# Moving the low parts of the weights to GpSimd, with a constant tensor for 1e-9 and one copy on ScalarE

## The chip, the cores and the metric

The kernel runs on one core of one Trainium2 chip. The metric is the device time of one launch in microseconds (us); lower is better. A core has TensorE (PE in the profile) for matrix products, VectorE (DVE), ScalarE (ACT) and GpSimd (POOL) for element-wise work, and SyncE (SP), which here issues the DMA transfers. Each engine works through its own instructions in order; semaphores make one engine wait for another. SBUF is the on-chip memory that all engines use, PSUM the memory that TensorE writes its results to.

## The reference

```python
# 8 batches, 8 heads, 576 rows, head size 64
k_p = k.reshape(8, 8, 72, 8, 64).mean(axis=3)      # keys pooled by 8
v_p = v.reshape(8, 8, 72, 8, 64).mean(axis=3)
scores = (1 / sqrt(64)) * q @ k_p.transpose(0, 1, 3, 2)
scores = scores - max(scores, axis=-1, keepdims=True)
attn = exp(scores)
attn = attn / (sum(attn, axis=-1, keepdims=True) + 1e-09)
x = (attn @ v_p)                                   # rearranged to 4608 x 512
h = x @ w_in                                       # 512 x 2048
g = maximum(0.01 * h, h)
out = g @ w_out                                    # 2048 x 512, float32
```

The two weights arrive as 64-bit floats. The kernel makes 32-bit values of them on the chip, and it keeps nearly the whole float32 precision in its matrix products by splitting each operand into a high part (rounded to TensorE's fp32r format) and a low part (what the rounding left).

## The kernel before, in words

**Tiling.** The 4608 rows of x are nine chunks of 512 rows. The hidden width of 2048 is sixteen groups f of 128. For a chunk and a group, twelve matmuls build h in a PSUM tile `ph` (L851 high weight by high x, L852 high weight by low x, L853 low weight by high x, four times each). ScalarE applies the leaky relu to it (L856) and rounds it to `gh` (L859), VectorE subtracts for the low part `gl` (L860), and twelve more matmuls add g times the second weight to four output tiles `acc` (L877, L878, L879). The second product of a group comes two groups after the first.

**Attention.** A tile of 128 rows of q is transposed by TensorE to `pq` (L467) and copied from PSUM to `qT` (for the first batch by VectorE at L470 where the tile number t is above 1, by ScalarE at L472 otherwise). `pss` (L495) holds scores of four heads; VectorE takes the row maximum (L503, into the tile `red`), ScalarE the exponentials and their sums (L505, `e`), VectorE adds 1e-9 to the sums and takes the reciprocal (L516 and L517 in `norm_unit` for the first three batches, L535 and L536 in `norm_via` for the rest), and GpSimd multiplies (L519, L523, L539, L545; `at`). TensorE transposes this (`pp`, L587), ScalarE and VectorE split it in parts (`pT_hi` L589, `pT_rem` L590, `pT_lo` L593, L597), and TensorE multiplies with the pooled v (`pa`, L612 to L615). The low part of v that belongs to it, and `kT`, the pooled keys (L405 and L406), come once for a batch. GpSimd does the pooling sums of later batches (L254, L261) on the raw tiles that SyncE's queue loads; the rows that don't fit a tile go through `kremraw` and `vremraw` to `v_parts` (L433 on ScalarE, L434 on VectorE).

**Weights.** There are 32 conversions: for each group f one of the first weight (i = 0) and one of the second (i = 1), each of 128 partitions by 512 values. `head` reads the two halves of the 64-bit words from SBUF: ScalarE rescales them in place (L198, L199), and VectorE puts the result together in a tile `w_t` with three instructions (L200, L201, L204). `tail` then has ScalarE write the rounded high part (L208) and VectorE the low part, `w_t` minus the high part (L209). The tile `w_t` lies in PSUM while the list `banks` has more than one entry, which is so for the first six conversions (f = 0, 1, 2), and in SBUF in a pool of three buffers for the other 26. The steps of the next conversion come between the head and the tail of one, and a conversion's `bits` go on to the DMA of a group four later (`stage`). The conversions come in stretches: the first six with the first batch's attention, the next 13 (f = 3 to 8, and one of f = 9) up to and beside the first pass over chunk 0, and the other 13 beside the second half of chunk 1 and what follows it.

**What sets the order.** TensorE's order is written out by hand: the string `FIRST` for the first batch, and then a loop over `runs` (chunk 0 with groups 0 to 7, the two halves of chunk 1 with groups 0 to 7, chunk 1 with groups 8 to 15, chunk 0 with groups 8 to 15, and then each chunk with all groups), which spreads the attention of the following batches and the steps of the conversions between the matmuls. The other engines get their order from a scheduler, which works with estimated times; a changed estimate or engine can therefore also change the order of instructions that the edit doesn't name.

Of the kernel before, what the change touches and what calls it, by code (L numbers as in the profile page):

```python
# [10 lines left out]
F32 = mybir.dt.float32  # L11
# [4 lines left out]
ALU = mybir.AluOpType  # L16
# [8 lines left out]
def tile_pooled_attention_ffn(  # L25
# [9 lines left out]
    nc = tc.nc  # L35

    P = 128
# [36 lines left out]
    const = ctx.enter_context(tc.tile_pool(name="const", bufs=1))  # L74
# [63 lines left out]
        "rem": const.tile([P, PMAX], F32R, name="pT_rem"),  # L138
    }

    warm = const.tile([P, 1], F32, name="warm")
    nc.gpsimd.memset(warm, 0.0)
    nc.scalar.activation(warm, warm, AF.Exp)
# [11 lines left out]
    def spare(f, i, shape, dtype, name):  # L155

        return wts.tile(shape, dtype, tag=f"w{i}_{f}", name=name)

    def stage(f):

        if f >= NF:
            return
        slot = NF - 1 if f == NF - 2 else NF - 1 - f % SPARE
        for i in range(2):
            shape = [P, DM, 2]
            if slot > f:
                t = spare(slot, i, shape, I32, f"w{i}_bits{f}")
            else:
                t = two.tile(shape, I32, tag="raw", name=f"w{i}_bits{f}")
            if i == 0:  # L170
                nc.sync.dma_start(
                    t.rearrange("p (k f) w -> p k f w", k=NK), w_in[:, :, f * P : (f + 1) * P, :]
                )
            else:
                nc.sync.dma_start(t, w_out[:, f, :, :])
            bits[i, f] = t

    def convert(i, f):

        st = {}  # L180

        def head():
            b = bits.pop((i, f))
            low, high = b[:, :, 0], b[:, :, 1]
            ws[i, f] = spare(f, i, [P, 2, DM], F32R, f"w{i}_{f}")

            if len(banks) > 1:
                k = 2 + (2 * f + i) % 2
                t = ps_acc.tile([P, DM], I32, tag=f"acc{k}", name=f"w{i}_t{f}")
            else:  # L190
                t = five.tile([P, DM], I32, tag="o", name=f"w{i}_t{f}")
            st["w"] = t.bitcast(F32)

            after = casts[-BEHIND] if len(casts) >= BEHIND else anchor.get("act")
            with tc.issue_after(after.ins) if after else nullcontext():
                nc.scalar.mul(high.bitcast(F32), high.bitcast(F32), 2.0**-112)  # L198
                nc.scalar.activation(low, low.bitcast(U32), AF.Copy, scale=2.0**-29)  # L199
            nc.vector.tensor_scalar(t, high, -0x80000000, None, op0=ALU.bitwise_and)  # L200
            nc.vector.scalar_tensor_tensor(  # L201
                t, high, 3, t, op0=ALU.logical_shift_left, op1=ALU.bitwise_or
            )
            nc.vector.tensor_tensor(t, t, low, op=ALU.add)  # L204

        def tail():
            w, t = ws[i, f], st["w"]
            nc.scalar.copy(w[:, 0, :], t)  # L208
            nc.vector.tensor_tensor(w[:, 1, :], t, w[:, 0, :].bitcast(F32), op=ALU.subtract)  # L209
            if i == 1:  # L210
                stage(f + SPARE)

        return head, tail

    banks = [(ps_a, "a"), (ps_a, "a"), (ps_h, "h"), (ps_h, "h")]
# [229 lines left out]
    def q_tile(b, t):  # L447
        qT = two.tile([P, NK, P], F32, tag="qT", name=f"qT{b}_{t}")
        if tiles[b][t][1] < P:
            nc.gpsimd.memset(qT[:, :, tiles[b][t][1] :], 0.0)  # L450
        return qT

    def q_unit(b, t, qr):
        n = tiles[b][t][1]
        if b > 1:

            qT = q_tile(b, t)
            m = n // 32
            blocks = qr.rearrange("a h d -> a (h d)")[:, : NK * n]
            nc.vector.transpose(  # L460
                qT[:, :, :n].rearrange("k p (s g) -> k g p s", g=m),
                blocks.rearrange("a (g p d) -> a g p d", g=m, p=NK),
            )
            return qT
        pq = bank(b, f"pq{b}_{t}")
        for p in range(NK):
            nc.tensor.transpose(pq[:, p, :n], qr[:n, 2 * p : 2 * p + 2, :], ident[:n, :n])  # L467
        qT = q_tile(b, t)
        if b == 0 and t > 1:
            nc.vector.tensor_copy(qT[:, :, :n], pq[:, :, :n])  # L470
        else:
            nc.scalar.copy(qT[:, :, :n], pq[:, :, :n])  # L472
        return qT
# [6 lines left out]
    def wide_at(b, t, nm):  # L480
        return b == 0 and (nm, t) in WIDE
# [31 lines left out]
    def norm_unit(b, t, g, e, sm):  # L513
        n = tiles[b][t][1]
        eng = nc.vector if b == 0 and t in NORM_DVE else nc.gpsimd
        nc.vector.tensor_scalar_add(sm[:n], sm[:n], 1e-9)  # L516
        nc.vector.reciprocal(sm[:n], sm[:n])  # L517
        at = wide(b, t, g, "at", [3, P]) if wide_at(b, t, "at") else three.tile([P, 3, P], F32, tag="at", name=f"at{b}_{t}_{g}")
        eng.tensor_tensor(  # L519
            at[:n, 0:2, :].rearrange("a i (h s) -> a (i h) s", h=2), e[:n, :, 0:MAIN],  # L520
            sm[:n].unsqueeze(2).broadcast_to([n, 4, MAIN]), op=ALU.mult,
        )
        ins = eng.tensor_tensor(  # L523
            at[:n, 2, :].rearrange("a (h c s) -> a h c s", h=4, c=4),
            e[:n, :, MAIN:].unsqueeze(2).broadcast_to([n, 4, 4, REM]),
            sm[:n].unsqueeze(2).unsqueeze(3).broadcast_to([n, 4, 4, REM]), op=ALU.mult,
        )
        if b == 0:
            anchor[eng] = ins
        return at  # L530

    def norm_via(b, t, g, e, sm):

        n = tiles[b][t][1]
        nc.vector.tensor_scalar_add(sm[:n], sm[:n], 1e-9)  # L535
        nc.vector.reciprocal(sm[:n], sm[:n])  # L536
        at = three.tile([P, 4, 3, 32], F32, tag="at", name=f"at{b}_{t}_{g}")
        for i in range(2):
            nc.gpsimd.tensor_tensor(  # L539
                at[:n, :, i, :].rearrange("a (h f) j -> a h f j", h=2),  # L540
                e[:n, 2 * i : 2 * i + 2, 0:MAIN].rearrange("a h (f j) -> a h f j", f=2),
                sm[:n, 2 * i : 2 * i + 2].unsqueeze(2).unsqueeze(3).broadcast_to([n, 2, 2, 32]),
                op=ALU.mult,
            )
        nc.gpsimd.tensor_tensor(  # L545
            at[:n, :, 2, :].rearrange("a h (c s) -> a h c s", c=4),
            e[:n, :, MAIN:].unsqueeze(2).broadcast_to([n, 4, 4, REM]),
            sm[:n].unsqueeze(2).unsqueeze(3).broadcast_to([n, 4, 4, REM]), op=ALU.mult,
        )
        rows = dram.tile([4, n, 96], F32, name=f"rows{b}_{t}_{g}")  # L550
        nc.sync.dma_start(
            rows.rearrange("x a y -> a x y"), at[:n].rearrange("a x i j -> a x (i j)")
        )
        return rows
# [518 lines left out]
```

## Time and profile before

| | |
|---|---|
| time, median of 3 runs | 936.06 us (935.46 to 937.29) |
| the profiled execution, its own time | 936.69 us |
| its span, first to last instruction | 934.9 us |
| TensorE (PE) busy | 903.4 us, 97% of the span |
| VectorE (DVE) busy | 424.9 us, 45% |
| ScalarE (ACT) busy | 417.2 us, 45% |
| GpSimd (POOL) busy | 183.9 us, 20% |
| mean granted TensorE clock | 0.991 |

The profile is of one execution; 1.8 us of its time lie outside the span. "Busy" counts the time in which an engine had an instruction under way. In the timelines a row has the start of the first instruction in us, the time taken in us, the engine, the line of the kernel and the operation, what is written and read, the shape, and how many instructions of the kind the row joins ("x2"). In brackets, where there is one, stands how long the engine was idle before it, and what it waited for. A "PEld" row is the load of a stationary operand, an "SPq" row the issue of a transfer. The granted clock is a share of TensorE's full speed.

### The profile page before, as it was taken

The numbers are of one execution on the slowest core, as the hardware profiler recorded it, in microseconds if no ns is written. First come the engines' busy times: TensorE is split into PE (matmuls) and PEld (weight loads), VectorE is DVE, ScalarE is ACT, GpSimd is POOL, SyncE is SP. The second block draws the span as 40 slices with busy tenths as digits, with TensorE's granted clock in tenths as the row PEclk, the third lists the DMA queues.
The fourth block names the chain that finished last, engine by engine and source line by source line (L and its number), as shares of the span: only waits on it lengthen the run. The fifth ranks groups of instructions, "written<-read, shape, count | busy, mean of one in ns | idle before, by whom it ended". The sixth has DMA issues, their size and how long they took to land.

```text
span 934.9 us, 12770 instructions
## 1 busy us (share of the span) xinstructions
PE 903.4 (97%) x4364; PEld 757.0 (81%) x4364; DVE 424.9 (45%) x986; ACT 417.2 (45%) x1375; POOL 183.9 (20%) x354
## 2 busy tenths in 40 slices
PE   5599999999999999999999999999999999999998
PEld 4478888888888888888888888888888888888886
DVE  6999469435343453436235534454345422421111
ACT  5788567435343444434344434443544333323221
POOL 4501110355023500313023212420211011000000
PEclk9799999999999999999999999999999999999999
DMA  9955231245032422514144404421322011101001
GB/s 264 320 181 169 61 76 46 52 116 143 12 96 53 108 72 54 125 35 110 33 90 115 107 7 106 98 71 32 102 50 61 26 62 31 39 1 46 1 1 45
DMA packets 127328, 75.14 MB, mean 80 GB/s; under 512 B 93472, under 2 KB 112672, under 8 KB 127264
## 3 DMA queue, kind: packets, MB, share of 16 engines
q1 hardware_dynamic: 127120, 74.21, 30.2%
q8 instruction: 34, 0.56, 0.2%
q14 instruction: 30, 0.25, 0.1%
q10 hardware_dynamic: 144, 0.13, 0.0%
HBM read 54.98 MB, written 19.33 MB: 79 GB/s over the span
## 4 chain that ended last, share of the span: by engine, by line
PE 86%; ACT 3%; DVE 3%; DMA 2%; POOL 1%; issue 1%; SPq 0%; POOLq 0%; DVEq 0%; ACTq 0%
PE acc L877 13%; PE acc L879 13%; PE acc L878 13%; PE ph L851 13%; PE ph L853 13%; PE ph L852 13%; PE pss L495 4%; PE pa L615 1%; PE pa L612 1%; PE pa L613 1%; PE pa L614 1%; ACT e L505 1%; PE pp L587 1%; DMA blocks<-rows 1%; DMA k0raw<-in_k_dram 0%
## 5 line engine op out<-in xcount | busy, mean ns | idle before, releaser
L851 PE MATMUL ph<-xh,w 128*128 128x512 f32 (+1 forms) x608 | 235.6, 387 | 0.1
L853 PE MATMUL ph<-xh,w 128*128 128x512 f32 (+1 forms) x608 | 231.1, 380 | 0.0
L852 PE MATMUL ph<-xl,w 128*128 128x512 f32 (+1 forms) x608 | 230.7, 379 | 0.0
L877 PE MATMUL acc<-w,gh 128*128 128x512 f32 x576 | 230.3, 400 | 0.0
L879 PE MATMUL acc<-w,gl 128*128 128x512 f32 x576 | 225.1, 391 | 0.0
L878 PE MATMUL acc<-w,gh 128*128 128x512 f32 x576 | 224.8, 390 | 0.0
L856 ACT ACTIVATE ph<-ph 128x512 f32<-128x512 f32 (+1 forms) x152 | 85.4, 562 | 263.3 <-PE ph L853 263.1
L860 DVE TENSOR_TENSOR gl<-ph,gh 128x512 fp32r<-128x512 f32 (+1 forms) x152 | 100.2, 659 | 224.8 <-ACT gh L859 224.2
L505 ACT ACTIVATE e<-pss,red 128x72 f32<-128x72 f32 (+1 forms) x320 | 98.2, 322 | 96.9 <-DVE red L503 96.8
L853 PEld LDWEIGHTS ph<-xh,w 128*128 128x128 f32 x608 | 114.5, 188 | 22.0
L851 PEld LDWEIGHTS ph<-xh,w 128*128 128x128 f32 x608 | 114.8, 189 | 20.8 <-DVE gl L860 0.5
L852 PEld LDWEIGHTS ph<-xl,w 128*128 128x128 f32 x608 | 114.8, 189 | 20.0
L879 PEld LDWEIGHTS acc<-w,gl 128*128 128x128 f32 x576 | 108.1, 188 | 23.3
L877 PEld LDWEIGHTS acc<-w,gh 128*128 128x128 f32 x576 | 108.3, 188 | 20.4
L878 PEld LDWEIGHTS acc<-w,gh 128*128 128x128 f32 x576 | 108.3, 188 | 20.0
L539 POOL TENSOR_TENSOR at<-e,red 128x128 f32<-128x128 f32 (+1 forms) x100 | 37.9, 400 | 320.1 <-DVE red L536 177.4
L859 ACT CAST gh<-ph 128x512 fp32r<-128x512 f32 (+1 forms) x152 | 86.0, 566 | 4.0
L503 DVE TENSOR_REDUCE red<-pss 128x4 f32<-128x288 f32 (+1 forms) x80 | 36.2, 453 | 81.0 <-PE pss L495 78.1
L505 ACT ACTIVATION_READ_ACCUMULATOR e<-pss,red 128x1 f32 (+1 forms) x320 | 65.8, 206 | 0.0
L495 PEld LDWEIGHTS pss<-kT,qT 128*128 128x128 f32 x320 | 50.0, 195 | 9.8 <-DVE qT L470 4.2
L495 PE MATMUL pss<-kT,qT 128*128 128x144 f32 x320 | 53.4, 293 | 3.8 <-DVE qT L470 3.8
L567 DVE STREAM_TRANSPOSE pp<-blocks 128x384 f32<-128x384 f32 (+1 forms) x50 | 36.5, 760 | 37.1 <-DMA blocks<-rows 36.7
(120 smaller groups left out, 822.0 us busy)
## 6 DMA issues: line engine op xcount, KB each, us to landing
out_dram<-o SPq DMA_DIRECT2D x34, 256.0 KB, 2.4
w_bits<-in_moe_w_in_dram SPq DMA_DIRECT2D x16, 512.0 KB, 10.5
w_bits<-in_moe_w_out_dram SPq DMA_DIRECT2D x16, 512.0 KB, 4.9
rows<-at SPq DMA_DIRECT2D x40, 192.0 KB, 3.1
blocks<-rows SPq DMA_DIRECT2D x40, 192.0 KB, 2.6
q<-in_q_dram SPq DMA_DIRECT2D x96, 64.0 KB, 2.5
k0raw<-in_k_dram SPq DMA_DIRECT2D x12, 256.0 KB, 3.9
k1raw<-in_k_dram SPq DMA_DIRECT2D x12, 256.0 KB, 3.8
```

The costliest lines, as they stand in the source:

```text
L495: nc.tensor.matmul(sc[:, 2 * SP * i : 2 * SP * (i + 1)], qT[:, p, :], kT[:, p, :, :].rearrange("d i s -> d (i s)"), start=True, stop=True,)
L505: ins = nc.scalar.activation(e[:n, h, :], scv[:n, h, :], AF.Exp, bias=mx[:n, h : h + 1], accum_out=sm[:n, h : h + 1],)
L539: nc.gpsimd.tensor_tensor(at[:n, :, i, :].rearrange("a (h f) j -> a h f j", h=2), e[:n, 2 * i : 2 * i + 2, 0:MAIN].rearrange("a h (f j) -> ...
L851: nc.tensor.matmul(ph, w[:, 0, ks], xh[kk][:, r], start=kk == 0, stop=False)
L852: nc.tensor.matmul(ph, w[:, 0, ks], xl[kk][:, r], start=False, stop=False)
L853: nc.tensor.matmul(ph, w[:, 1, ks], xh[kk][:, r], start=False, stop=kk == NK - 1)
L856: nc.scalar.activation(ph, ph, AF.Prelu, alpha=0.01)
L859: casts.append(nc.scalar.copy(gh, ph))
L860: nc.vector.tensor_tensor(gl, ph, gh.bitcast(F32), op=ALU.subtract)
L877: nc.tensor.matmul(a, gh[:, r], hi, start=first, stop=False)
L878: nc.tensor.matmul(a, gh[:, r], lo, start=False, stop=False)
L879: nc.tensor.matmul(a, gl[:, r], hi, start=False, stop=last)
```

## The change

There are three edits.

1. The low part of a weight (L209) is subtracted by GpSimd where `w_t` lies in SBUF, by VectorE where it lies in PSUM. This moves 26 of 32 instructions of 128 by 512 from VectorE to GpSimd.
2. A constant tile `tiny` of 128 by 4 is filled with 1e-9 at the start by GpSimd, and the 80 additions of 1e-9 (30 at L516, 50 at L535) become an addition of two tensors in place of a tensor and a number.
3. The copy of q's transpose of the first batch's last tile (t = 4, 64 rows) goes to ScalarE (L472) in place of VectorE (L470). Tiles 2 and 3 stay on VectorE.

```diff
+    tiny = const.tile([P, 4], F32, name="tiny")
+    nc.gpsimd.memset(tiny, 1e-9)
...
             ws[i, f] = spare(f, i, [P, 2, DM], F32R, f"w{i}_{f}")
 
+            st["eng"] = nc.vector if len(banks) > 1 else nc.gpsimd
             if len(banks) > 1:
                 k = 2 + (2 * f + i) % 2
                 t = ps_acc.tile([P, DM], I32, tag=f"acc{k}", name=f"w{i}_t{f}")
...
             nc.scalar.copy(w[:, 0, :], t)
-            nc.vector.tensor_tensor(w[:, 1, :], t, w[:, 0, :].bitcast(F32), op=ALU.subtract)
+            st["eng"].tensor_tensor(w[:, 1, :], t, w[:, 0, :].bitcast(F32), op=ALU.subtract)
...
-        if b == 0 and t > 1:
+        if b == 0 and 1 < t < 4:
             nc.vector.tensor_copy(qT[:, :, :n], pq[:, :, :n])
         else:
             nc.scalar.copy(qT[:, :, :n], pq[:, :, :n])
...
-        nc.vector.tensor_scalar_add(sm[:n], sm[:n], 1e-9)
+        nc.vector.tensor_tensor(sm[:n], sm[:n], tiny[:n], op=ALU.add)
```

The last pair of lines stands twice, at L516 and L535. The lines of the changed kernel lie four further down than those of the kernel before (L209 is L213, L503 is L507, L856 is L860); the text uses the numbers of before unless it says otherwise. The orders of TensorE and SyncE are the same in both kernels. The others change at several places, of which three are shown. Names such as `w_3_603` are the tile (the weight part of group 3) and a running number that differs by two between the kernels.

The first place is VectorE's and ScalarE's order around the copy of q, some 45 us into the program. VectorE before:

```order
L204 ISA w_t_565<-w_bits_179,w_t_565 128x1024
L630 TENSOR_TENSOR xl_2_403<-pa_1_2_536,xh_2_399 128x256
L434 SCALAR_TENSOR_TENSOR v_parts<-vremsum_164,v_parts 32x64 x2
L200 TENSOR_SCALAR w_t_514<-w_bits_177 128x512
L470 COPY qT_4_559<-pq_4_554 128x4x64
L630 TENSOR_TENSOR xl_3_404<-pa_1_3_541,xh_3_400 128x256
L209 TENSOR_TENSOR w_2_564<-w_t_565,w_2_564 128x512
L201 SCALAR_TENSOR_TENSOR w_t_514<-w_bits_177,w_t_514 128x512
L503 TENSOR_REDUCE red_4_0_577<-pss_4_0_573 64x4
```

ScalarE of the changed kernel there, and behind it VectorE of the changed kernel:

```order
L633 CAST xh_2_401<-pa_1_2_536 128x256
L437 ACTIVATE v_parts<-vremsum_166 32x64 x2
L633 CAST xh_3_402<-pa_1_3_543 128x256
L476 COPY qT_4_561<-pq_4_556 128x4x64
L212 CAST w_2_566<-w_t_567 128x512
L509 ACTIVATE e_4_0_578,red_4_0_579<-pss_4_0_575,red_4_0_579 64x72 x4
```

```order
L204 TENSOR_SCALAR w_t_516<-w_bits_179 128x512
L634 TENSOR_TENSOR xl_3_406<-pa_1_3_543,xh_3_402 128x256
L213 TENSOR_TENSOR w_2_566<-w_t_567,w_2_566 128x512
L507 TENSOR_REDUCE red_4_0_579<-pss_4_0_575 64x4
L205 SCALAR_TENSOR_TENSOR w_t_516<-w_bits_179,w_t_516 128x512
```

The copy has left VectorE's row and stands on ScalarE directly behind the last `xh`, ahead of the cast of `w_2`. On VectorE the maximum `red_4_0` has moved ahead of the conversion's L201.

The second place is where the subtractions of groups 3 and 4 now stand on GpSimd, between the multiplications of the first batch and those of the second. GpSimd before:

```order
L519 TENSOR_TENSOR at_4_1_600<-e_4_1_586,red_4_1_587 64x256
L523 TENSOR_TENSOR at_4_1_600<-e_4_1_586,red_4_1_587 64x128
L519 TENSOR_TENSOR at_0_0_829<-e_0_0_793,red_0_0_794 128x256
L523 TENSOR_TENSOR at_0_0_829<-e_0_0_793,red_0_0_794 128x128
L519 TENSOR_TENSOR at_0_1_925<-e_0_1_867,red_0_1_868 128x256
```

GpSimd of the changed kernel:

```order
L523 TENSOR_TENSOR at_4_1_602<-e_4_1_588,red_4_1_589 64x256
L527 TENSOR_TENSOR at_4_1_602<-e_4_1_588,red_4_1_589 64x128
L213 TENSOR_TENSOR w_3_605<-w_t_606,w_3_605 128x512
L213 TENSOR_TENSOR w_3_618<-w_t_619,w_3_618 128x512
L213 TENSOR_TENSOR w_4_666<-w_t_667,w_4_666 128x512
L213 TENSOR_TENSOR w_4_717<-w_t_718,w_4_717 128x512
L523 TENSOR_TENSOR at_0_0_831<-e_0_0_795,red_0_0_796 128x256
L527 TENSOR_TENSOR at_0_0_831<-e_0_0_795,red_0_0_796 128x128
L213 TENSOR_TENSOR w_6_878<-w_t_879,w_6_878 128x512
```

Four subtractions stand ahead of the multiplication `at_0_0`, where nothing stood before.

The third place is the pooling of the third batch's keys on GpSimd, and ScalarE's order at its end. GpSimd before, and of the changed kernel:

```order
L254 TENSOR_TENSOR k0raw_2002<-k0raw_2002 128x2x128
L261 TENSOR_TENSOR ksum_2001<-k0raw_2002 128x256
L254 TENSOR_TENSOR k1raw_2008<-k1raw_2008 128x2x256
L254 TENSOR_TENSOR kremraw_2014<-kremraw_2014 64x256
L254 TENSOR_TENSOR k1raw_2008<-k1raw_2008 128x2x128
L254 TENSOR_TENSOR kremraw_2014<-kremraw_2014 64x128
L261 TENSOR_TENSOR ksum_2001<-k1raw_2008 128x256
```

```order
L258 TENSOR_TENSOR k0raw_2004<-k0raw_2004 128x2x128
L213 TENSOR_TENSOR w_15_2111<-w_t_2112,w_15_2111 128x512
L265 TENSOR_TENSOR ksum_2003<-k0raw_2004 128x256
L258 TENSOR_TENSOR k1raw_2010<-k1raw_2010 128x2x256
L258 TENSOR_TENSOR k1raw_2010<-k1raw_2010 128x2x128
L258 TENSOR_TENSOR kremraw_2016<-kremraw_2016 64x256
L265 TENSOR_TENSOR ksum_2003<-k1raw_2010 128x256
```

The last subtraction of the weights stands ahead of the sum `ksum` of `k0raw`, and the sums of `k1raw` stand together. ScalarE before, and of the changed kernel, where the chain ends:

```order
L424 ACTIVATE v_hi<-vsum_2019 64x4x64 x2
L856 ACTIVATE ph_14_2150<-ph_14_2150 128x512
L433 ACTIVATE v_parts<-vremsum_2020 32x64 x2
L859 CAST gh_14_2164<-ph_14_2150 128x512
L654 CAST xh_0_2217<-x_tail 128x128
```

```order
L428 ACTIVATE v_hi<-vsum_2021 64x4x64 x2
L437 ACTIVATE v_parts<-vremsum_2022 32x64 x2
L860 ACTIVATE ph_14_2152<-ph_14_2152 128x512
L863 CAST gh_14_2166<-ph_14_2152 128x512
L658 CAST xh_0_2219<-x_tail 128x128
```

`v_parts` and the leaky relu of `ph_14` have changed places.

More of the change, by code (lines that the diff above doesn't have):

```diff
@@ L534, in norm_via @@
         n = tiles[b][t][1]
-        nc.vector.tensor_scalar_add(sm[:n], sm[:n], 1e-9)
+        nc.vector.tensor_tensor(sm[:n], sm[:n], tiny[:n], op=ALU.add)
         nc.vector.reciprocal(sm[:n], sm[:n])
```

## The prediction

> **What bounds the kernel now.** I read the shares of the engines first, then the windows (for each stretch the busy us of the engines with their number of instructions; at the end granted clock, share of the DMA engines and GB/s), and then what TensorE waits for.
>
> ```profile
> PE 903.4 (97%) x4364; PEld 757.0 (81%) x4364; DVE 424.9 (45%) x986; ACT 417.2 (45%) x1375; POOL 183.9 (20%) x354
> ...
> 50.00:60.00 10.00, 8.90 (x43) 6.32 (x42) 8.96 (x21) 10.00 (x27) 1.75 (x4) 0.97 0.51 155
> 60.00:70.00 10.00, 9.24 (x52) 7.64 (x53) 9.74 (x21) 8.04 (x21) 0.00 (x0) 1.00 0.65 191
> 140.00:160.00 20.00, 20.00 (x129) 18.16 (x128) 18.93 (x36) 16.99 (x36) 0.00 (x0) 1.00 0.18 53
> ```
>
> TensorE is full over most of the span, so an edit to another engine is worth only what it does to TensorE's waits. These lie early, where the averages of 45% and 20% mislead: between 50 and 70 us VectorE is nearly full and GpSimd nearly idle. What TensorE waits for from 50 to 97 us stands in the first fence (us in total, times, longest), the largest entry from 96 us to the end in the second:
>
> ```profile
> PE pa L612 <- ACT e L505: 0.9, 1, 0.9
> PE pq L467 <- DVE kT L406: 0.8, 1, 0.8
> PE pa L613 <- DVE pT_lo L593: 0.7, 1, 0.7
> PE pa L612 <- ACT pT_hi L589: 0.2, 1, 0.2
> ```
>
> ```profile
> PE pa L612 <- ACT e L505: 1.8, 2, 0.9
> ```
>
> So the gain after 50 us is capped at some 2.6 us (0.9 + 0.8 + 0.7 + 0.2), while a new delay of VectorE has no such cap.
>
> **Edit 3, the copy of q.** It stands in the middle of TensorE's largest wait of this part:
>
> ```profile
> 43.90 0.59 ACT L208 CAST w<-w_t 128x512 fp32r<-128x512 f32 x1 [0.74 <-DVE w_t L204]
> 45.45 0.42 DVE L470 COPY qT<-pq 128x256 f32<-128x256 f32 x1
> 45.79 0.41 DVE L630 TENSOR_TENSOR xl<-pa,xh 128x256 fp32r<-128x256 f32 x1
> 45.92 1.94 PEld L495 LDWEIGHTS pss<-kT,qT 128*128 128x128 f32 x8 [3.16 <-DVE qT L470]
> 46.12 0.68 DVE L209 TENSOR_TENSOR w<-w_t,w 128x512 fp32r<-128x512 f32 x1
> 46.72 0.69 DVE L201 SCALAR_TENSOR_TENSOR w_t<-w_bits,w_t 128x512 int32<-128x512 int32 x1
> 47.31 0.44 DVE L503 TENSOR_REDUCE red<-pss 64x4 f32<-64x288 f32 x1
> 47.79 0.32 ACT L505 ACTIVATE e<-pss,red 64x72 f32<-64x72 f32 x1 [3.30 <-DVE red L503]
> ```
>
> In the changed order ScalarE copies right behind the last `xh`, in the 0.74 us in which it was idle before 43.90. Its own copy of this size takes 0.37 us in the row below, so `qT` is there by about 43.5 and `pss` starts some 2.3 us earlier.
>
> ```profile
> L472 ACT COPY qT<-pq x7: 374/586/595, 10.7 to 113.3; 128x512 f32<-128x512 f32 x6, 128x256 f32<-128x256 f32 x1
> ```
>
> What follows does not come 2.3 us earlier. The maximum L503 is late next: it stands behind `xl` and one L209 on VectorE. It loses the copy's 0.34 (45.45 to 45.79) and the L201's 0.59 (46.72 to 47.31) ahead of it, 0.93 together. `e` moves by this, and from there ScalarE has no gap (10.00 of 10 us in the window from 50), so its parts of the next products (L612, L613) come 0.93 earlier as well. That is the edit's worth if nothing behind it binds: at the least 0, at the most the 2.3.
>
> **Edit 1, the subtractions.** What VectorE does between 57 and 95 us, by lines (count, busy us, mean ns, idle before), the window of the same stretch, what an instruction of this size costs on GpSimd (min/median/max ns), and, in the fence behind it, what happens when both run:
>
> ```profile
> L209 DVE TENSOR_TENSOR w<-w_t,w 128x512 fp32r<-128x512 f32 x13 | 9.6, 742 | 0.7 <-ACT w L208 0.7
> L204 DVE CUSTOM_DVE_ANT_0 w_t<-w_bits,w_t 128x1024 uint16<-128x1024 uint16 x11 | 7.6, 702 | 0.2
> L201 DVE SCALAR_TENSOR_TENSOR w_t<-w_bits,w_t 128x512 int32<-128x512 int32 x11 | 7.6, 690 | 0.1
> L200 DVE TENSOR_SCALAR w_t<-w_bits 128x512 int32<-128x512 int32 x10 | 4.4, 446 | 0.2
> ...
> 57.00:95.00 38.00, 36.88 (x193) 30.29 (x192) 36.41 (x77) 31.88 (x89) 4.93 (x8) 1.00 0.56 172
> ...
> L254 POOL TENSOR_TENSOR k0raw<-k0raw x13: 736/1281/1307, 25.1 to 532.4; 128x512 f32<-128x512 f32 x7, 128x256 f32<-128x256 f32 x6
> ```
>
> ```profile
> 71.20 0.61 POOL L519 TENSOR_TENSOR at<-e,red 128x256 f32<-128x256 f32 x1 [18.72 <-ACT w L208]
> 71.78 0.85 POOL L523 TENSOR_TENSOR at<-e,red 128x128 f32<-128x128 f32 x1
> ...
> 71.22 1.15 DVE L209 TENSOR_TENSOR w<-w_t,w 128x512 fp32r<-128x512 f32 x1 [0.18 <-ACT w L208]
> ...
> 29.44 1.27 POOL L254 TENSOR_TENSOR v0raw<-v0raw 128x512 f32<-128x512 f32 x1 [0.61 <-DMA v0raw<-in_v_dram]
> ...
> 30.22 0.68 DVE L204 CUSTOM_DVE_ANT_0 w_t<-w_bits,w_t 128x1024 uint16<-128x1024 uint16 x1
> ```
>
> One subtraction frees about 0.60 us of VectorE (L209 at 46.12, the next at 46.72) and costs GpSimd 1.28. GpSimd has room, but the two do not run freely beside each other. L209, with both inputs in SBUF, took 1.15 us beside L519, and L523 behind it took longer too. L204 kept 0.68 beside the 1.27 of L254; there `w_t` was still in PSUM. So a running GpSimd instruction makes VectorE wait where both its inputs are in SBUF, which holds for all remaining L201 and L204. I count L200 with them, which reads one tensor; without it the share below falls from 58% to 46%. [...]
>
> Those three lines are 7.6 + 7.6 + 4.4 = 19.6 us, or 16.7 without the 0.09 by which each of the 32 overlaps the next instruction (0.69 long, 0.60 apart); VectorE has 36.41 - 13 * 0.60 = 28.6 us left there without L209, so they are 58%. If a GpSimd instruction meets VectorE at random, it stops it for 0.58 * 1.28 = 0.74 us, more than the 0.60 saved. I take the two places where TensorE notices:
>
> ```profile
> 59.50 0.29 DVE L593 TENSOR_TENSOR pT_lo<-pp,pT_hi 128x128 fp32r<-128x128 f32 x1
> ...
> 62.22 0.68 DVE L209 TENSOR_TENSOR w<-w_t,w 128x512 fp32r<-128x512 f32 x1
> ...
> 65.07 0.43 DVE L406 TENSOR_SCALAR kT<-pk 64x256 f32<-64x256 f32 x1
> ...
> 94.39 0.44 DVE L503 TENSOR_REDUCE red<-pss 128x4 f32<-128x288 f32 x1
> ```
>
> *kT at 65 us.* L593 waits for ScalarE and so comes 0.93 earlier; from there to L406 one L209 goes. Without a collision kT is 1.53 earlier, with two whole ones (the second subtraction of group 3, the first of group 4) 1.53 - 2 * 1.28 = -1.03, that is later. I take one by its share (0.74) and a third of another (0.35): 0.4 earlier. TensorE then leaves its wait at kT 0.4 earlier, and the rest of the 0.93 is lost.
>
> *The wait of 0.9 at 95 us.* L503 is late there behind VectorE's queue. Ten subtractions between 67 and 95 us free 6.0 us and bring 12.8 on GpSimd: by 58% 7.4 us of stops, 1.4 us later. With three buffers for `w_t`, the last three can run behind the stretch; then seven stop it by 5.2, 0.8 us earlier. I take the middle, 0.3 later. The bounds are 0.9 earlier (the wait gone) and 6.8 later (every stop whole).
>
> [...]
>
> **What else moves.** At the end of the last stretch the new order puts a subtraction ahead of `ksum`, and `v_parts` ahead of a leaky relu that was long done. The last row, of the page's groups, is TensorE's load of weights, which once waited 0.5 us for `gl`; that was here:
>
> ```profile
> 178.87 0.74 POOL L261 TENSOR_TENSOR ksum<-k0raw 128x256 f32<-128x256 f32 x1
> ...
> 182.91 0.74 POOL L254 TENSOR_TENSOR kremraw<-kremraw 64x256 f32<-64x256 f32 x1 [1.50 <-DMA kremraw<-in_k_dram]
> ...
> 184.72 0.73 POOL L261 TENSOR_TENSOR ksum<-k1raw 128x256 f32<-128x256 f32 x1
> ...
> 196.21 0.57 ACT L856 ACTIVATE ph<-ph 128x512 f32<-128x512 f32 x1
> ...
> 199.10 0.54 ACT L433 ACTIVATE v_parts<-vremsum 32x64 fp32r<-32x64 f32 x2 [2.32 <-POOL vremsum L261]
> ...
> L851 PEld LDWEIGHTS ph<-xh,w 128*128 128x128 f32 x608 | 114.8, 189 | 20.8 <-DVE gl L860 0.5
> ```
>
> `ksum` and with it the transfer and sum of `kremraw` come 1.28 later, but the second sum of `k1raw` is done by then, so the `ksum` at 184.72 moves by 0.2 only (182.91 + 1.28 + 0.74 = 184.93), and all behind it. Then the relu of 0.5 us stands behind `v_parts`, and `gh`, `gl` and TensorE behind that. I take 0.7 us of new wait at 201 us (0.2 + 0.5); the bounds are 0 and 1.9 (the 1.28 in full).
>
> From 138 to 177 us, TensorE waits for nothing; the 13 subtractions there bring 16.6 us on GpSimd, which fit into 39 only if their stops fall where VectorE has room. I take 0, and keep it as a rival.
>
> **Edit 2, tiny.** The addition of four values takes this (min/median/max ns):
>
> ```profile
> L516 DVE TENSOR_SCALAR red<-red x30: 128/166/721, 15.2 to 280.9; 128x4 f32<-128x4 f32 x24, 64x4 f32<-64x4 f32 x6
> ```
>
> Its longest, 721 against 166, shows that it waits for something in its present form; with two inputs in SBUF I expect the same of the new one, as of L209. The bounds are 0.55 us less or more for each. From 50 us on no wait of TensorE in the fences above is for the multiplications behind it, so I take 0. One more fill at the start lies beside the first loads.
>
> **Sum.** -0.4 + 0.3 + 0.7 = +0.6 us on the profiled execution's 936.69, so 937.3; that lay 0.63 above the median of 936.06, so **936.7** against the runs shown. A measurement of this kernel can't tell less than 0.2% (1.9 us) from no change, which makes this "no change".
>
> **The rivals.** *GpSimd fits into the gaps:* its instructions meet VectorE where that reads PSUM or waits, kT comes 1.53 earlier, the wait at 95 us goes (0.9), the order at 201 us costs nothing: -2.4, that is 933.6. For it speaks that VectorE's load falls by 7.8 of 36.41 us; against it that L200, L201 and L204 stand one behind the other. *The collisions decide:* VectorE between 57 and 95 us gets slower as soon as more than 6.0 of the 12.8 us stop it (47%). With kT 1.03 later, 1.4 at 95 us and 0.7 at 201 us it is +3.1, so 939.2. [...] Against it stands that both engines then wait and the next subtractions come further apart. *The last stretch slips:* VectorE is busy 18.93 of 20 us there; one stop of 1.28 that isn't made up moves the pooling chain, and 201 us costs 1.9 in place of 0.7: 936.06 + 0.6 + 1.2 = 937.9, and more with each further stop.
>
> **How the numbers follow.** Forecast, within 0.2%: 0.37, its own range 934.2 to 937.9. Gaps: 0.33, all of it faster. Collisions 0.20 and last stretch 0.10: slower, 0.30. The range of 8 in 10 goes from the full gain, 933.4, to a little above the collisions' time, 939.8.
>
> **What would show it.** `qT` at about 43.5 us on ScalarE with the wait at L495 below 1 us; L406 at 64.2 to 65.2; L201 and L204 with times of 0.7 to 2.0 us beside GpSimd rows of 1.28 between 57 and 95 us; a wait at L612 of 1 to 2 us near 95; TensorE waiting 0.7 us more at 201. Unstretched L201 and L204 would prove the collisions wrong, and a new wait of TensorE for the low part of a weight (L853 or L878) the whole sum.

## The result and the profile after

The changed kernel takes 941.08 us (median of 6 runs, 939.77 to 942.77) against 936.03 (6 runs) for the kernel before. The ratio is 1.0052, with a 95% interval from 1.0042 to 1.0063: half a per cent slower, outside the predicted range of 933.4 to 939.8.

TensorE executes the same 4364 matmuls in the same order in both kernels, so the start of one matmul in both profiles shows how far the change is ahead or behind at that point:

| matmul | before, us | after, us | difference |
|---|---|---|---|
| first one | 6.04 | 5.94 | -0.10 |
| `pss` behind the moved copy | 45.92 | 43.12 | -2.80 |
| `pa` of the second pieces | 59.85 | 57.87 | -1.98 |
| `pss` near 92 us | 92.85 | 91.60 | -1.25 |
| `pa` behind the wait at 95 us | 96.30 | 96.59 | +0.29 |
| `ph` a little later | 98.81 | 100.68 | +1.87 |
| `ph` behind the wait at 201 us | 201.03 | 205.00 | +3.97 |
| `pk` a little later | 204.22 | 209.70 | +5.48 |
| last one | 930.65 | 935.20 | +4.55 |

The change leads by 2 us at 60 us; 1.24 us of this lead are there already at the last matmul before the moved copy (42.64 before, 41.40 after). It loses at two places: 3.9 us between 90 and 101, and 3.6 us between 201 and 210. Nothing is lost in the 700 us behind.

The first fence has the entries of TensorE's waits after the change (waited for, us in total, times, longest) that are new or longer from 50 us on; of the 3.0 us for `gl`, 2.1 are at 205 us. Before, the wait for `gl` was 0.5 us and that for `e` at 95 us 0.9.

```profile
PE ph L855 <- DVE gl L864: 3.0, 2, 2.1
PE pa L616 <- ACT e L509: 1.8, 2, 1.6
PE pq L471 <- DVE kT L410: 1.1, 1, 1.1
PE pa L616 <- DVE red L521: 0.5, 1, 0.5
PE pss L499 <- ACT e L509: 0.5, 1, 0.5
```

The waits alone don't make up the loss. The windows of the changed kernel (busy us of the engines, then the granted clock, DMA share and GB/s) show why:

```profile
96.00:102.00 6.00, 5.41 (x20) 4.42 (x21) 1.76 (x6) 1.71 (x8) 1.52 (x3) 0.72 0.12 41
204.00:210.00 6.00, 5.00 (x18) 4.03 (x18) 2.94 (x6) 2.68 (x8) 4.14 (x4) 0.72 0.35 90
```

Behind each of the two waits TensorE's granted clock is below full, 0.72 on the mean. In the timeline a matmul of 512 columns goes from 0.23 to 0.43 us apart, from 97.48 to 100.68 and from 206.51 to 209.95:

```profile
205.00 0.50 PE L855 MATMUL ph<-xh,w 128*128 128x512 f32 x1 [2.14 <-DVE gl L864]
...
206.51 0.62 PE L855 MATMUL ph<-xh,w 128*128 128x512 f32 x1
206.93 0.63 PE L856 MATMUL ph<-xl,w 128*128 128x512 f32 x1
```

VectorE got less work, and its instructions got longer. These are its conversion lines of the changed kernel between 57 and 95 us; before, the means were 690 (L205), 702 (L208) and 446 ns (L204):

```profile
L205 DVE SCALAR_TENSOR_TENSOR w_t<-w_bits,w_t 128x512 int32<-128x512 int32 x10 | 9.1, 914 | 0.1
L208 DVE CUSTOM_DVE_ANT_0 w_t<-w_bits,w_t 128x1024 uint16<-128x1024 uint16 x10 | 8.9, 900 | 0.2
L204 DVE TENSOR_SCALAR w_t<-w_bits 128x512 int32<-128x512 int32 x10 | 5.8, 587 | 0.4 <-POOL w L213 0.2 <-issue 0.2
...
57.00:95.00 38.00, 35.88 (x188) 29.47 (x186) 33.14 (x62) 29.68 (x84) 18.74 (x19) 1.00 0.53 158
```

In all VectorE is busy 33.14 us there in place of 36.41. So what TensorE lost at 95 us can't be read from that sum. The maxima in VectorE's queue (L503 before, L507 after) show where the lead went: at 72.88 the maximum came 1.87 us earlier than before and at 80.70 1.50 earlier, but at 89.59 it came 0.23 later and at 94.68 0.29 later. A part of the freed time was spent idle, since VectorE then had to wait for ScalarE. These are the changed kernel's longest idle times of VectorE between 69 and 77 us; before, all idle times there add up to 0.6 us:

```profile
70.88 0.69 DVE L864 TENSOR_TENSOR gl<-ph,gh 128x512 fp32r<-128x512 f32 x1 [1.50 <-ACT gh L863]
74.78 0.16 DVE L520 TENSOR_TENSOR red<-red,tiny 128x4 f32<-128x4 f32 x1 [0.85 <-ACT e L509]
76.99 0.86 DVE L431 SCALAR_TENSOR_TENSOR v_lo<-pvm,v_hi 64x256 fp32r<-64x256 f32 x2 [1.10 <-ACT v_hi L428]
```

Then three subtractions follow each other on GpSimd from 87.84 on, and VectorE's conversion instructions beside them, ahead of the maximum L507 that TensorE needs, take 1.58, 1.15 and 1.64 us:

```profile
87.84 4.40 POOL L213 TENSOR_TENSOR w<-w_t,w 128x512 fp32r<-128x512 f32 x3 [0.90 <-ACT w L212]
...
88.09 1.58 DVE L208 CUSTOM_DVE_ANT_0 w_t<-w_bits,w_t 128x1024 uint16<-128x1024 uint16 x1
...
89.96 1.15 DVE L204 TENSOR_SCALAR w_t<-w_bits 128x512 int32<-128x512 int32 x1
91.14 1.64 DVE L205 SCALAR_TENSOR_TENSOR w_t<-w_bits,w_t 128x512 int32<-128x512 int32 x1
...
94.68 0.45 DVE L507 TENSOR_REDUCE red<-pss 128x4 f32<-128x288 f32 x1
```

The first of these three rows costs 0.9 us. The other two cost 1.7 us, about what the three subtractions took that stood on VectorE there before (3 * 0.60), so this bunch undoes its own relief and 0.8 us more.

In the late stretch the same happens once in each step. A conversion of the kernel before, first, came every 2.82 us (L204 at 147.74 and 150.56); after the change it is 3.10 (L208 at 150.18 and 153.28), since GpSimd's subtraction runs until 151.20 and L208 takes 1.57 us in place of 0.69, a stop of 0.88:

```profile
147.74 0.69 DVE L204 CUSTOM_DVE_ANT_0 w_t<-w_bits,w_t 128x1024 uint16<-128x1024 uint16 x1
150.56 0.69 DVE L204 CUSTOM_DVE_ANT_0 w_t<-w_bits,w_t 128x1024 uint16<-128x1024 uint16 x1
```

```profile
150.18 1.57 DVE L208 CUSTOM_DVE_ANT_0 w_t<-w_bits,w_t 128x1024 uint16<-128x1024 uint16 x1
153.28 1.57 DVE L208 CUSTOM_DVE_ANT_0 w_t<-w_bits,w_t 128x1024 uint16<-128x1024 uint16 x1
...
149.38 1.82 POOL L213 TENSOR_TENSOR w<-w_t,w 128x512 fp32r<-128x512 f32 x1 [1.28 <-ACT w L212]
```

### The profile page after: what moved, and what is told of

The parts are those of the page before. It is cut to its first block, busy times and chain, and to the rows that moved or that the text cites. A ratio compares the mean times of both kernels' runs of the same rounds, so it can differ in the third digit from the quotient of the medians.

```text
span 939.3 us, 12792 instructions
## 1 busy us (share of the span) xinstructions
PE 906.9 (97%) x4364; PEld 759.3 (81%) x4364; DVE 420.9 (45%) x959; ACT 418.0 (45%) x1376; POOL 222.3 (24%) x381
## 4 chain that ended last, share of the span: by engine, by line
PE 85%; DVE 4%; ACT 3%; DMA 2%; POOL 1%; issue 1%; SPq 0%; DVEq 0%; POOLq 0%; ACTq 0%
PE ph L855 13%; PE acc L881 13%; PE ph L857 13%; PE ph L856 13%; PE acc L883 13%; PE acc L882 13%; PE pss L499 3%; DVE w_t L205 1%; DVE w_t L208 1%; PE pa L616 1%; PE pa L617 1%; PE pa L619 1%; PE pa L618 1%; DVE w_t L204 1%; PE pp L591 1%
## 5 line engine op out<-in xcount | busy, mean ns | idle before, releaser
L856 PE MATMUL ph<-xl,w 128*128 128x512 f32 (+1 forms) x608 | 231.8, 381 | 0.0
L860 ACT ACTIVATE ph<-ph 128x512 f32<-128x512 f32 (+1 forms) x152 | 85.5, 562 | 259.5 <-PE ph L857 259.3
L856 PEld LDWEIGHTS ph<-xl,w 128*128 128x128 f32 x608 | 115.5, 190 | 20.3
L507 DVE TENSOR_REDUCE red<-pss 128x4 f32<-128x288 f32 (+1 forms) x80 | 36.3, 453 | 83.3 <-PE pss L499 80.0
```

What stands on the lines that cost most here:

```text
L856: nc.tensor.matmul(ph, w[:, 0, ks], xl[kk][:, r], start=False, stop=False)
L860: nc.scalar.activation(ph, ph, AF.Prelu, alpha=0.01)
```

## The experiments

Theory A: the loss comes from GpSimd's subtractions stopping VectorE's instructions. Rival B: it comes from the earlier copy of q. Rival C: it comes from the new form of the addition. A further rival blames the changed order or the longer way to the low part. Each kernel ran 4 to 11 times, beside the kernel before on the same chip; the ratio and its 95% interval are the measure, and 0.1% is 0.94 us. Line numbers shift by a few from kernel to kernel, so go by the names of the tiles. What a single profile shows is one execution.

| kernel | median, us | before, us | ratio (95%) |
|---|---|---|---|
| e1_copy | 935.28 | 936.28 | 0.9989 (0.9980 to 0.9998) |
| e2_sub | 942.60 | 936.28 | 1.0066 (1.0053 to 1.0078) |
| e3_tiny | 935.00 | 936.28 | 0.9985 (0.9976 to 0.9993) |
| e4_early | 937.93 | 936.28 | 1.0011 (1.0002 to 1.0020) |
| e5_late | 935.67 | 936.62 | 0.9994 (0.9985 to 1.0003) |
| e6_both | 934.00 | 936.62 | 0.9972 (0.9962 to 0.9982) |
| e7_tile | 935.21 | 936.62 | 0.9985 (0.9977 to 0.9994) |
| e8_beside | 945.89 | 936.62 | 1.0096 (1.0083 to 1.0110) |
| e9_warm | 939.20 | 936.26 | 1.0033 (1.0020 to 1.0045) |
| e10_half | 934.11 | 936.26 | 0.9981 (0.9972 to 0.9990) |
| e11_fill | 936.32 | 936.26 | 1.0000 (0.9991 to 1.0009) |
| e12_pad | 934.79 | 936.26 | 0.9985 (0.9976 to 0.9994) |
| e13_mid | 936.59 | 936.70 | 1.0000 (0.9991 to 1.0008) |
| e14_quarter | 936.00 | 936.70 | 0.9991 (0.9982 to 1.0000) |
| e15_pad64 | 937.41 | 936.70 | 1.0006 (0.9997 to 1.0015) |

### Each edit alone, and two together

The edit of e1_copy:

```diff
-        if b == 0 and t > 1:
+        if b == 0 and 1 < t < 4:
```

> Only edit 3, the copy of q on ScalarE; the subtractions and the 1e-9 are as before. Theory A (the loss comes from the subtractions on GpSimd): TensorE keeps the 1 to 2 us that the changed kernel had gained at 60 us, since nothing takes it back at 95 and 201 us: 934.0 to 935.3, ratio 0.998 to 0.999. Rival B (the earlier copy shifts the first stages so that a wait of TensorE ends in another place and costs clock): 937 or more.

e2_sub has only the choice of engine for the subtraction:

```diff
-            nc.vector.tensor_tensor(w[:, 1, :], t, w[:, 0, :].bitcast(F32), op=ALU.subtract)
+            st["eng"].tensor_tensor(w[:, 1, :], t, w[:, 0, :].bitcast(F32), op=ALU.subtract)
```

> Only edit 1, the 26 subtractions on GpSimd. Theory A: the whole loss and without the copy's gain, 941 to 943, with new waits of TensorE near 95 and 201 us and half the clock for 2 to 4 us behind each. Rival B: the loss belongs to the copy's shift, so this stays within 1 us of 936.

e3_tiny has the tile and both additions:

```diff
+    tiny = const.tile([P, 4], F32, name="tiny")
+    nc.gpsimd.memset(tiny, 1e-9)
-        nc.vector.tensor_scalar_add(sm[:n], sm[:n], 1e-9)
+        nc.vector.tensor_tensor(sm[:n], sm[:n], tiny[:n], op=ALU.add)
```

> Only edit 2, 1e-9 as a constant tensor, 80 additions of two tensors. Theory A: nothing, 935.5 to 936.6; VectorE's additions take 0.15 to 0.17 us as before, and up to 1.1 beside GpSimd in both forms. Rival C (the form with a number does not wait for GpSimd and the one with two tensors does): some of the 30 additions of the first batches get longer and it is slower by 0.5 to 2 us.

e6_both has the edits of e1_copy and e3_tiny.

> Edits 2 and 3 without the subtractions. If the gains of the copy (-1.0) and of tiny (-1.3) add up, 934.0; if they fill the same wait, 934.8 to 935.3. In either case below both kernels, with no half clock behind 50 us.

The copy alone is 0.11% faster and tiny alone 0.15%; together they are 0.28% faster, so they add up, and e6_both is faster than both kernels. The subtractions alone are 0.66% slower; in that profile the clock is below full behind the wait at 201 us, as expected (0.89 on the mean from 200 to 215 us), but stays full behind the one at 95 us (1.00 from 90 to 105). Against e6_both they cost the changed kernel 0.80% (1.0052 - 0.9972), 7.5 us. Theory A holds on what is to blame, and rivals B and C fall: copy and tiny are gains.

### Each stretch alone

e4_early keeps the changed kernel but for the later 13 subtractions, e5_late but for the earlier 13 (the comment behind a line names its kernel):

```diff
-            st["eng"] = nc.vector if len(banks) > 1 else nc.gpsimd
+            st["eng"] = nc.vector if len(banks) > 1 or (f, i) > (9, 0) else nc.gpsimd     # e4_early
+            st["eng"] = nc.vector if len(banks) > 1 or (f, i) <= (9, 0) else nc.gpsimd    # e5_late
```

> The changed kernel, but only the 13 subtractions up to the first of group 9 go to GpSimd; the later 13 stay on VectorE. Theory A: the loss at 95 us stays (about +3.5 us with its half clock), that at 201 us goes (-3.6 with its half clock): 937 to 938.5. [...]

> The changed kernel, but only the 13 late subtractions (second of group 9 and on) go to GpSimd; the early 13 stay on VectorE. Theory A (each stretch costs by itself): no new wait at 95 us, the wait and the half clock at 201 us stay, +3.5 on copy and tiny together (about 934): 937 to 938.5. If the late loss only came from the early stretch's delay, it is 934 to 935.

Against e6_both (0.9972), the early stretch costs 0.39%, 3.7 us, and the late one 0.22%, 2.1 us: 5.8 of the 7.5. In e4_early TensorE is 1.92 us behind the kernel before at 99 us, as in the changed kernel, and loses nothing at 201. Its eleven executions fall into two groups: the three with a mean granted clock of 0.993 took 935.57 to 936.24 us, the eight with 0.989 to 0.991 took 937.20 to 938.39. The profile is one of 0.989, with the lower clock behind the wait at 95 us (0.89 on the mean from 90 to 105 us); where the others had theirs isn't recorded.

e5_late came out below its range (935.67 against 937 to 938.5): the wait at 201 us is there with 2.04 us, but in this profile (934.99 us, of 934.98 to 937.63) the clock stays full behind it. First TensorE's row, then the window:

```profile
200.57 0.50 PE L855 MATMUL ph<-xh,w 128*128 128x512 f32 x1 [2.04 <-DVE gl L864]
...
200.00:212.00 12.00, 11.43 (x56) 9.63 (x57) 5.85 (x13) 6.14 (x22) 7.29 (x10) 1.00 0.35 95
```

So one and the same wait of 2 us was followed by a lower clock in one kernel and not in another.

### What the lower clock costs

e9_warm adds nine matmuls to the changed kernel in front of that wait. Their product isn't used, so the kernel does more work than it needs:

```diff
+        if n == REST and f == fs0[n]:
+            keep = ps_a.tile([P, NK, P], F32, tag="a", name="keep").rearrange("p a b -> p (a b)")
+            for _ in range(9):
+                nc.tensor.matmul(keep[:, :w_], w[:, 0, 0:P], xh[0][:, r], start=True, stop=True)
```

> The changed kernel with nine extra matmuls of 512 columns (about 2 us, into a PSUM tile that nobody reads) right before TensorE's wait for gl at 201 us, so that it works through the wait; it does more and useless work. If the half clock behind that wait costs 1.5 us of its own, it goes and the time falls to 939.4 to 940.2. If the wait alone costs and the clock record is only a by-product, 941 to 941.5.

It is 0.19% faster than the changed kernel (1.0052 to 1.0033), 1.8 us and a little more than expected, by doing useless work. The two intervals just touch, but its slowest execution (939.54) is below the changed kernel's fastest (939.77). Its timeline and window:

```profile
202.71 2.20 PE L856 MATMUL keep<-xh,w 128*128 128x512 f32 x9
204.75 0.43 PE L860 MATMUL ph<-xh,w 128*128 128x512 f32 x1
...
196.00:212.00 16.00, 16.00 (x76) 13.21 (x75) 5.80 (x14) 5.70 (x16) 9.61 (x13) 1.00 0.31 80
```

`ph` starts no later (204.75 against 205.00), and the clock stays at 1.00. The lower clock behind the wait at 201 us is thus a cost of its own. With it the account comes to 3.7 + 2.1 + 1.8 = 7.6 of the 7.5 us. That it fits so closely is partly luck, as each of the three is known to about 1 us only.

### What GpSimd does to VectorE

e8_beside is the kernel before, and beside the 13 late subtractions on VectorE GpSimd does each again, into a tile that nothing reads in that stretch:

```diff
             nc.vector.tensor_tensor(w[:, 1, :], t, w[:, 0, :].bitcast(F32), op=ALU.subtract)
+            if (f, i) > (9, 0):
+                again = pT["hi"].rearrange("p i x -> p (i x)")[:, :DM]
+                nc.gpsimd.tensor_tensor(again, t, w[:, 0, :].bitcast(F32), op=ALU.subtract)
```

> The kernel before, and beside VectorE's 13 late subtractions GpSimd does the same subtraction again into a tile that nobody reads there. No product moves and VectorE's order in this stretch is the old one, so only what GpSimd's running does to VectorE is added. Theory A (a running GpSimd instruction with SBUF inputs stops VectorE's): the step of one conversion grows from 2.82 us to 3.4 to 4.1, the pooling starts 5 us or more later, and it is 941 or more. Rival (the loss comes from GpSimd's longer way to the low part and from the order of the products): VectorE's instructions keep their times, and it is 936 to 937.

The ratio is 1.0096. In the timeline L209 takes 1.79 us in place of 0.69, the step is 3.71 us (149.30 to 153.01), and TensorE waits for `gl`, which stands behind this on VectorE, at five places by 3.1 us in all, 0.63 of them at 152.09 (its sixth and longest such wait has 3.8):

```profile
149.30 1.79 DVE L209 TENSOR_TENSOR w<-w_t,w 128x512 fp32r<-128x512 f32 x1
153.01 1.79 DVE L209 TENSOR_TENSOR w<-w_t,w 128x512 fp32r<-128x512 f32 x1
...
152.09 0.39 PE L854 MATMUL ph<-xh,w 128*128 128x256 f32 x1 [0.63 <-DVE gl L863]
```

The low part that is used still comes from VectorE, and VectorE's order is the old one throughout. Apart from the added instructions, ScalarE's and GpSimd's orders are the old ones too until 176 us; behind that `v_parts` again stands ahead of a leaky relu. By 170 us this profile has already lost 4.8 us (0.5 ahead of the kernel before at 140, 4.3 behind at 170). So the stop by a running GpSimd instruction is enough for a loss without any change of order. The kernel frees nothing on VectorE, so its loss is larger than that of the late stretch. The rival that blames the longer way falls: in the changed kernel, too, no wait of TensorE is for a weight's low part.

e10_half and e14_quarter cut each GpSimd subtraction of the changed kernel in two or four (the edit of the halves; the quarters are cut in the same way):

```diff
+            for h in ([slice(0, DM)] if st["eng"] is nc.vector else [slice(0, DM // 2), slice(DM // 2, DM)]):
+                st["eng"].tensor_tensor(w[:, 1, h], t[:, h], w[:, 0, h].bitcast(F32), op=ALU.subtract)
```

> The changed kernel with each GpSimd subtraction as two of 256 columns (about 0.73 us each in place of 1.28). [...] If GpSimd's total time decides (2 * 0.73 against 1.28), it is slower, 941 to 943.

> The changed kernel with each GpSimd subtraction as four of 128 columns (about 0.45 us each, 1.8 together in place of 1.28). If the length of one instruction decides what VectorE loses, it is about as with halves, 933.5 to 935. If GpSimd's total time decides, 936 to 939.

The time falls from 1.0052 to 0.9981 with halves (6.7 us, to 934.11, below the 941 to 943 that GpSimd's total time would give) and to 0.9991 with quarters, although GpSimd then works longer (two together in 1.44 us, at 70.55, or four in 1.71, at 68.95, in place of one in 1.26, at 95.28). The quarters' 936.00 us lies above the 933.5 to 935 that the length of one instruction alone would give, and at the lower end of what GpSimd's total time would. In their profile TensorE waits 1.5 us for `kT` at 65 us, where the halves have 0.7. The rows of the late stretch, first with halves, then with quarters, show L208 at 1.03 to 1.05 and at 0.73 us, in steps of 2.81 and 2.83:

```profile
148.87 1.03 DVE L208 CUSTOM_DVE_ANT_0 w_t<-w_bits,w_t 128x1024 uint16<-128x1024 uint16 x1
151.68 1.05 DVE L208 CUSTOM_DVE_ANT_0 w_t<-w_bits,w_t 128x1024 uint16<-128x1024 uint16 x1
```

```profile
147.33 0.73 DVE L208 CUSTOM_DVE_ANT_0 w_t<-w_bits,w_t 128x1024 uint16<-128x1024 uint16 x1
150.16 0.73 DVE L208 CUSTOM_DVE_ANT_0 w_t<-w_bits,w_t 128x1024 uint16<-128x1024 uint16 x1
```

In this stretch the stop goes with the length of one GpSimd instruction, not with GpSimd's total: it is 0.88, 0.35 and 0.04 us for L208, or 0.18 with quarters if the 0.14 is counted by which L205 is longer there. VectorE's, ScalarE's and GpSimd's orders are the same in e10_half and the changed kernel from 97 us on, so there the length is what differs. Between 80 and 96 us VectorE's and ScalarE's orders differ too, so what the halves gain at 95 us is not shown to come from the length.

The rows of the changed kernel at 150 us show the stop on both sides: GpSimd's subtraction starts 0.66 us before VectorE's L205 ends (149.38 and 150.04) and takes 1.82 us, 0.54 longer than 1.28, and L208, 0.69 long by itself, takes 1.57 and ends 0.55 us behind that subtraction.

e13_mid looks for a use of this. It has edits 2 and 3 and, in halves, only the seven subtractions between 70 and 95 us on GpSimd:

```diff
+            st["eng"] = nc.vector if len(banks) > 1 or f < 6 or (f, i) > (9, 0) else nc.gpsimd
```

> Edits 2 and 3, and only the seven subtractions between 70 and 95 us (groups 6, 7, 8 and the first of 9) on GpSimd, each as two of 256 columns. If short instructions there only fill gaps, VectorE's queue is shorter, the wait of 0.9 us at 95 us goes and the lead of 2.4 us that edits 2 and 3 have at 76 us is kept: 933.0 to 933.6, the best of all. If any subtraction on GpSimd costs VectorE as much as it frees, it is no better than edits 2 and 3 alone, 934.0, or worse.

It is at 1.0000, worse than e6_both, and its wait for `e` near 95 us is 2.3 us. In its timeline six halves of three subtractions run together right in front of that place, as three whole ones do in the changed kernel:

```profile
87.60 5.35 POOL L214 TENSOR_TENSOR w<-w_t,w 128x256 fp32r<-128x256 f32 x6 [0.36 <-ACT w L212]
```

In e10_half, where the wait is 0.2, four, two and four halves stand at 83.54, 89.24 and 93.38, apart from each other. So halves alone don't prevent the loss at this place. That the bunch decides it is argued from these profiles; no run moved it alone. No kernel with subtractions on GpSimd came out faster than e6_both; e10_half's interval overlaps with that of e6_both.

### Where the gain of the tile comes from

Edit 2 was put at nothing and gained 0.15%. e7_tile has the tile and its fill and keeps the old additions, e11_fill has one more fill of the old tile `warm` and no new tile, and e12_pad and e15_pad64 have a tile of 4 and of 16 values that nothing writes or reads:

```diff
+    tiny = const.tile([P, 4], F32, name="tiny")      # e7_tile
+    nc.gpsimd.memset(tiny, 1e-9)                     # e7_tile
+    nc.gpsimd.memset(warm, 0.0)                      # e11_fill
+    pad = const.tile([P, 4], F32, name="pad")        # e12_pad
+    pad = const.tile([P, 16], F32, name="pad")       # e15_pad64
```

> The tile tiny and its fill alone; the additions of 1e-9 keep their number. If the gain of edit 2 comes from the tile's presence (other places of the tiles behind it in SBUF, the first transfer of k1raw landing 0.6 us earlier), 935.0 as with the whole edit. If it comes from the form of the addition, 936.0 to 936.3.

> The kernel before with one more fill of the tile warm on GpSimd, no new tile. If the gain of the tile tiny comes from the extra instruction, 935.0; if from the place of the tiles behind it, 936.2 as before.

> The kernel before with a tile of four values that nothing writes or reads: the same instructions in the same order, all tiles behind it 16 bytes further in SBUF. If the gain of the tile tiny comes from the places, 935.0 with k1raw landing 0.5 us earlier; if from the extra instruction, 936.2.

> The kernel before with an unused tile of 16 values, all tiles behind it 64 bytes further in SBUF. If any shift frees the first transfers, 934.8 as with 16 bytes; if the place modulo 64 bytes decides, 936.2 as before.

The tile alone gains the whole 0.15%, the unused tile of 16 bytes too; the fill alone and the 64 bytes gain nothing. So it is neither the form of the addition nor the instruction, but that the tiles behind lie 16 bytes further on. The profiles show it in the first transfers. VectorE's first row on `k1raw` in the kernel before, in e12_pad, e11_fill and e15_pad64, in this order:

```profile
6.94 0.69 DVE L254 TENSOR_TENSOR k1raw<-k1raw 128x512 f32<-128x512 f32 x1 [0.95 <-DMA k1raw<-in_k_dram]
```

```profile
6.23 0.69 DVE L256 TENSOR_TENSOR k1raw<-k1raw 128x512 f32<-128x512 f32 x1 [0.45 <-DMA k1raw<-in_k_dram]
```

```profile
6.95 0.69 DVE L255 TENSOR_TENSOR k1raw<-k1raw 128x512 f32<-128x512 f32 x1 [1.01 <-DMA k1raw<-in_k_dram]
```

```profile
6.84 0.69 DVE L256 TENSOR_TENSOR k1raw<-k1raw 128x512 f32<-128x512 f32 x1 [0.87 <-DMA k1raw<-in_k_dram]
```

Other profiles agree with this: with 16 bytes more this row starts at 6.18 us in e4_early, 6.29 in e3_tiny and 6.36 in the changed kernel, without them at 6.82 in e1_copy and 6.96 in e2_sub. The first stages, which wait for `k1raw`, come earlier with it: in e12_pad TensorE leads by 1.0 us at 18 us. Why a transfer is faster to such a place was not tried.

## Why the prediction was wrong

**Edit 3.** The mechanism was right, and so was the size where it counts. e6_both and e3_tiny differ by the copy alone. Through it `pss` starts 1.60 us earlier, not 2.3, because it then waits 1.57 us for `xl`; so the wait there didn't fall below 1 us. The products from 55 us on come 0.8 to 1.0 earlier, against 0.93 in the prediction, and at 74 us this is still there. Alone, the edit is worth 0.11%, 1.0 us.

**Edit 1, kT at 65 us.** I took 0.4 earlier. The 0.35 for "a third of another" is neither a third of 0.74 (0.25) nor of 1.28 (0.43), but this moves the term by 0.1 at most. In the changed kernel TensorE led by 2.02 us in front of this wait and by 1.70 behind it, a loss of 0.3 us where the prediction had 0.5 (0.93 - 0.4). This term was not where the loss came from.

**Edit 1, the wait at 95 us.** This is the first step that failed: "I take the middle, 0.3 later". TensorE went from 1.98 ahead to 0.29 behind, 2.3 us. This is inside the bounds I gave (0.9 earlier to 6.8 later), but beyond both values whose middle I took (0.8 earlier and 1.4 later). The last three subtractions did not run behind the stretch: nine of the ten ran ahead of the maximum, and the tenth stood behind it in both kernels (94.76 before, 95.28 after). With nine, the same sum would have given 9 * (0.74 - 0.60) = 1.3 later. The price of a collision was not too low: the three lines got longer by 10 * (0.22 + 0.20 + 0.14) = 5.6 us, against 7.4 in the sum. The 0.74 there, like the two whole collisions at kT, counts a stop at the whole 1.28 us of a GpSimd instruction. No run shows such a stop: the longest of L205 and L208 in the changed kernel are 0.96 and 0.97 us (1.65 and 1.67 in place of 0.69), and L209 of e8_beside has 1.10 in its rows (1.79 in place of 0.69). What the sum lacked is that time freed early was not kept: VectorE stood idle for 3.45 us in front of the three rows between 69 and 77 us, and the bunch from 87.84 on came behind that. How much of the 2.3 us each of the two is worth, no run separates.

**What else moves, at 201 us.** The second step that failed: "From 138 to 177 us [...] I take 0, and keep it as a rival". The rival was right. Each step from 147 us on took 0.28 us more (3.10 in place of 2.82), and the transfer of `k0raw` was issued at 175.58 in place of 171.31, 4.27 later, of which 1.9 were TensorE's own lateness. SyncE's rows of the kernel before and after:

```profile
171.31 2.13 SPq L277 DMA_DIRECT2D k0raw<-in_k_dram  x2
```

```profile
175.58 1.32 SPq L281 DMA_DIRECT2D k0raw<-in_k_dram  x2
```

The rest of this chain went as worked out. The `ksum` moved with the transfer (184.72 to 188.29, 3.57 for 3.67 on `k0raw`), and the leaky relu stood behind `v_parts`:

```profile
202.59 0.54 ACT L437 ACTIVATE v_parts<-vremsum 32x64 fp32r<-32x64 f32 x2 [2.83 <-POOL vremsum L265]
203.03 0.57 ACT L860 ACTIVATE ph<-ph 128x512 f32<-128x512 f32 x1
```

The wait was 2.1 us in place of the 0.7 in the prediction. e10_half separates the two parts: there ScalarE has the same order, but `v_parts` comes 1.5 us earlier in relation to TensorE, and the wait is 0.67 us. So the 0.7 for the order was about right, and the other 1.4 us are the slip of the late stretch that I had put at 0. No run has the full slip with the old order on ScalarE, so what the slip would cost by itself is not shown.

**What no term had.** The granted clock, the third step that failed. The prediction showed it in the windows and priced every wait by its length alone. Here it fell behind both waits: 1.6 us of TensorE's time at 97 us and 1.5 at 206 by the table of starts, and 1.8 us for the second by e9_warm. By these figures the loss without them would have been about 2 us, an estimate, and the time inside the range.

**Edit 2.** The prediction was right that the form of the addition costs nothing; that a tile of 16 bytes moves the tiles behind it, and that this is worth 1.4 us, was no step of it.

**The rivals.** The outcome is the two slower ones together, with the clock on top, but without the later kT of the first. I gave them 0.30 in all and priced them one at a time; both rest on the same stop, so I should have priced them together as well.

## What to carry to other kernels

An element-wise instruction moved from a full engine to an idle one isn't free when the two stop each other (here L208 took 1.57 us in place of 0.69 and the subtraction 1.82 in place of 1.28): look for rows in which they already stretch each other, and price the stop where the queue is read next, not as a mean over the stage. If the move is wanted all the same, try shorter instructions on the second engine: in the late stretch here they stopped L208 for less, by 0.35 us as halves and 0.04 as quarters in place of 0.88. And before a small gain is credited to an edit, put its tile in place without its use: 16 bytes of it gave 0.15%, as much as the edit.

## What the runs showed of the hardware

- A wait of TensorE of about 2 us cost almost as much again in one kernel and not in another. In the changed kernel matmuls were 0.43 us apart in place of 0.23 from 97.48 to 100.68, with a granted clock of 0.50 from 98 to 100 us, and from 206.51 to 209.95, with one of 0.52 from 208 to 210, behind a wait of 2.14; without this second wait e9_warm was 1.8 us faster. In e5_late a wait of 2.04 us was followed by a full clock (1.00 from 200 to 212). What decides between the two was not shown.
- Nine useless matmuls in a wait of TensorE, 2.20 us in all, made the changed kernel 0.19% faster, with a clock of 1.00 from 196 to 212 us (e9_warm).
- The transfer of `k1raw` at the start ends 0.7 us earlier when the tiles lie 16 bytes further in SBUF (6.94 to 6.23), and 0.1 us earlier with 64 bytes (6.84; e12_pad, e15_pad64).
- In the late stretch GpSimd instructions that take 0.74 us by themselves stopped VectorE's L208 by 0.35 us, those of 1.28 us by 0.88, and those of which four took 1.71 us by 0.04, with 0.14 more for L205 (e10_half, the changed kernel, e14_quarter).
